# Retention feeding a gated convolutional FFN: units shifted by one token, kept edge columns, one state product moved, and a new written-out order

## The chip, the cores and the metric

The kernel runs on one core of a Trainium2 chip. The metric is the device time of one execution in microseconds, from the core's start to the last output. The core has five engines that run side by side and meet only at semaphores: PE multiplies matrices (PEld is its loading of the stationary matrix), DVE and ACT do elementwise work, POOL does small elementwise work and issues some of the transfers, SP issues the others. Each engine takes its instructions strictly in the order of its queue.

## The reference

Two parts, one feeding the other. The first is retention: for each of 4 batches and 8 heads a 64x64 state is decayed and updated over 768 tokens. The second is a feed-forward net with a convolution of three tokens between its two matrix products.

```python
# retention: q, k, v are (4, 8, 768, 64)
for t in range(S):
    state = gamma * state + outer(k[:, :, t], v[:, :, t])
    y[:, :, t] = scale * einsum('bhd,bhde->bhe', q[:, :, t], state)
x = y.transpose(0, 2, 1, 3).reshape(B, S, H * D)       # (4, 768, 512)
# gated FFN: w_in (512, 1024), conv_w (3, 1024), w_out (1024, 512)
h = maximum(x @ w_in, 0.0)
conv_out[:, s] = sum_k conv_w[k] * h[:, s + k - 1]      # zero outside 0..767
gate = 1 / (1 + exp(-conv_out))
return h * gate @ w_out
```

Because of the convolution, output token s needs h of the tokens s-1, s and s+1.

## The kernel before, in words

**Groups, steps, units.** The four batches go in two groups of two. A group's 768 tokens are 12 steps of 64 tokens, so there are 24 steps; steps 0 to 11 are the first group and 12 to 23 the second. Three steps are a unit: 8 units of 192 tokens and two batches, four to a group. The two first steps are done in a form of their own (both batches of one 128-token piece, `WIDE`).

**A step n.** SP loads q, k, k with tokens first (`kt`) and v, 256 KB each, into one of four `rw` buffers, so the loads of step n can start only when step n-4 is done with its buffer. DVE scales q (`scale_q`, L527) and v (`scale_v`, L533; for early steps ACT does it, L552). One block on PE, `mix(n)`, then interleaves up to three sorts of 64x64 products, two of one sort and two of another in turn: the scores of step n+1 (into `ps_s`), the state's update by step n (into `ps_st`), and step n's output y (into `ps_yo`), which is one part for the first step of a group and two (masked scores times v, old state times q) for the others. Scores and state products use the two straight quadrants of the array ("straight"), y products the two crossed ones ("across"). DVE masks the scores (`masked`, L628), ACT copies the state into the next step's buffer (`carry`, L636). ACT and DVE split y into a rounded head and a rest (`x_head` L654, `x_rest` L659) in the unit's x tile `xu`, since each product of the net is made as three: head by head, head by rest, rest by head.

**A unit u.** For each of 8 column blocks f of w_in, PE makes h with 12 matmuls (`mm1(u, f)`, L738) into a `ps_m` bank, 388 columns wide: two batches of 192 tokens and one token on either side. To have those, each x tile holds 194 tokens; `halo` (L667, ACT) copies one column of x from the neighbouring unit's tile, and `x_tiles` (L643, POOL) writes zeros where the sequence ends. ACT takes h out of the bank with `relu` (L754) and multiplies by the middle tap (`conv_tap`, L767), DVE adds the two outer taps (`conv_side`, L772), ACT makes the sigmoid (`gate`), DVE multiplies (`gated`), and both split the result (`g_head`, `g_rest`) in a `g` tile. For each pair of blocks PE then makes its part of the output (`mm2`, L804, 6 matmuls of 512 columns for each of three 128-token tiles). ACT copies a tile out of its bank (`put`, L812) into one of four `t` buffers and POOL issues its transfer (`out`, L824); the last unit's go by SP. Unit 0 is computed before unit 1's first column of x is there, so `edge` (L759, ACT) later copies one column of h from unit 1 to unit 0.

**What sets the order.** A table of strings, `ORDER`, has one letter for each task of each engine, in the order in which the engine gets them; DMA is the order of loads on SP. `plan` replays these strings with estimated durations to hand out buffers and to place warming matmuls where PE would be idle early on; it changes no order within an engine. At most eight loads are under way (`fetch`, L450): each waits for the one eight before it to land.

Of the kernel before, what the change touches and what calls it, by code (L numbers as in the profile page):

```python
# [21 lines left out]
P = 128  # L22
C = 64
# [23 lines left out]

WIDE = 2
# [44 lines left out]
}  # L93
COLD = 6400
HOP, HOP_PE, SWITCH = 40, 65, (85, 190)
DMA_FIRST, DMA_BYTE, DMA_LAND, DMA_ISSUE, DMA_DEPTH = 1030, 1 / 395, 1030, 450, 8
FETCH, FETCH_NS, BEHIND, PACKET_LAG = (112.6, 126.6), (600, 2300), 500, {2: 700, 6: 1200, PE: 1000}
FIRST = {PE: 6700.0, DVE: 1200.0, ACT: 3200.0, POOL: 2500.0, DMA: 700.0}
# [31 lines left out]
def list_tasks():  # L130
# [22 lines left out]
    for n in range(N_STEPS):  # L153
# [19 lines left out]
        else:  # L173
# [13 lines left out]
            count = 32 + 32 * (c > 0) + 32 * both + 32 * (c + 1 < NC)  # L187
            pe(("mix", n), 1935, after, [("ps_yo", ("y", n))] + [("ps_s", n + 1)] * both, [("rw", n)], count)
        if n >= WIDE - 1 and c + 1 < NC:
            task(("carry", n), ACT, act(512, 45), [("state" if wide else "mix", n), ("load_q", n + 1)])  # L190
        if n == first:
            task(("x_tiles", u), POOL, (60, 120), [u and ("x_tiles", u - 1)], [("xu", u)])
        task(("x_head", n), ACT, act(512, 45), [("mix", n), ("x_tiles", u)])
        done = ("x_rest", n)
        task(done, DVE, tt(512), [("x_head", n)], free=[("ps_yo", ("y", n))])
        if n + 1 == first + width and c + 1 < NC:
# [718 lines left out]
```

## Time and profile before

| | |
|---|---|
| time, median of 3 runs | 347.95 us (347.15 to 348.5) |
| the profiled execution | 347.51 us, of which the span from first to last instruction is 345.8 us |
| PE busy | 335.7 us, 97% of the span |
| DVE, ACT, POOL busy | 205.3, 189.2, 18.4 us |
| granted TensorE clock | 1.00 |

The profile is of one execution. Its time is 0.44 us below the median of the runs, and 1.7 us of it lie outside the span. Busy is the time in which an engine has at least one instruction under way; matmuls overlap, so PE's busy share says that it is never without work for long, not that it works at its best rate. What ends its idle times is in the waits.

### The profile page before, as it was taken

How to read it: one execution, taken by the hardware profiler on the slowest of the kernel's cores; microseconds unless marked ns; L12 is line 12 of the kernel's file. 1: busy time of each engine (PE TensorE's matmuls, PEld its weight loads, DVE VectorE, ACT ScalarE, POOL GpSimd, SP SyncE). 2: the span in 40 equal slices, each digit the busy share in tenths (PEclk: the TensorE clock that was granted, in tenths of full speed). 3: DMA queues.
4: the chain of work that ended last, by engine and by line, in shares of the span. 5: the costliest groups of instructions: out<-in, count | busy, mean ns of one | idle time of the engine just before them, and what ended most of it. 6: DMA issues, size and time to landing. Idle time of an engine off the chain costs nothing.

```text
span 345.8 us, 9832 instructions
## 1 busy us (share of the span) xinstructions
PE 335.7 (97%) x4317; PEld 299.3 (87%) x4317; DVE 205.3 (59%) x318; ACT 189.2 (55%) x381; POOL 18.4 (5%) x45
## 2 busy tenths in 40 slices
PE   8789999999999999999999999999999999999996
PEld 5689899988989898889889988989899899998885
DVE  2756658887899875556921667834806641573540
ACT  1858997676775756365440667454327352453432
POOL 2000000000000001001000010020001000100200
PEclk9999999999999999999999999999999999999999
DMA  7988895766752322157005201020001000200203
GB/s 219 381 291 272 264 330 173 233 221 211 254 180 90 95 93 61 39 179 234 11 2 190 85 14 51 0 61 35 0 32 32 30 2 0 61 2 30 73 21 91
DMA packets 20935, 40.15 MB, mean 116 GB/s; under 512 B 2854, under 2 KB 3116, under 8 KB 20892
## 3 DMA queue, kind: packets, MB, share of 16 engines
q1 hardware_dynamic: 19100, 34.01, 29.5%
q0 software_dynamic: 1792, 5.51, 5.1%
q8 instruction: 34, 0.56, 0.6%
q14 instruction: 9, 0.07, 0.1%
HBM read 33.21 MB, written 6.29 MB: 114 GB/s over the span
## 4 chain that ended last, share of the span: by engine, by line
PE 85%; DMA 7%; SPq 2%; DVE 2%; issue 1%; ACT 1%; DVEq 0%; ACTq 0%
PE ps_yo L804 39%; PE ps_m L738 34%; PE ps_s L577 5%; PE ps_yo L577 4%; PE ps_st L577 4%; DMA rw<-in_qk 3%; SPq L450 2%; DMA w<-in_w_out 1%; DMA rw<-in_kv 1%; DMA w<-in_w_in 1%; DVE hc L772 1%; DVE rw L527 1%; ACT top L702 0%; ACT rw L552 0%; DVE g L791 0%
## 5 line engine op out<-in xcount | busy, mean ns | idle before, releaser
L738 PE MATMUL ps_m<-xu,w 128*128 128x388 f32 (+2 forms) x780 | 145.3, 339 | 0.5 <-issue 0.4
L804 PE MATMUL ps_yo<-w,g 128*128 128x512 f32 (+1 forms) x600 | 140.9, 386 | 0.1
L738 PEld LDWEIGHTS ps_m<-xu,w 128*128 128x128 f32 x780 | 136.2, 188 | 4.5 <-issue 0.6
L804 PEld LDWEIGHTS ps_yo<-w,g 128*128 128x128 f32 x600 | 108.6, 188 | 22.0 <-issue 0.4
L772 DVE SCALAR_TENSOR_TENSOR hc<-hc,cw_sb,hc 128x384 f32<-128x384 f32 x128 | 74.8, 612 | 59.9 <-ACT hc L767 58.6
L754 ACT ACTIVATE hc<-ps_m 128x388 f32<-128x388 f32 x64 | 31.1, 491 | 50.7 <-PE ps_m L738 48.6
L577 PE MATMUL ps_yo<-rw 64*64 64x64 f32 (+1 forms) x1408 | 47.8, 221 | 0.1
L577 PEld LDWEIGHTS ps_yo<-rw 64*64 64x64 f32 (+1 forms) x1408 | 43.9, 135 | 0.8 <-issue 0.5
L767 ACT ACTIVATE hc<-hc,cw_sb 128x384 f32<-128x384 f32 x64 | 38.3, 613 | 5.8 <-DVE g L791 5.6
L791 DVE TENSOR_TENSOR g<-hc,g 128x768 fp32r<-128x768 f32 x32 | 30.5, 953 | 17.9 <-ACT g L786 17.9
L786 ACT CAST g<-hc 128x768 fp32r<-128x768 f32 x32 | 26.5, 833 | 26.6 <-PE ps_yo L804 21.1
L782 DVE TENSOR_TENSOR hc<-hc,hc 128x768 f32<-128x768 f32 x32 | 30.3, 951 | 7.4 <-ACT hc L777 7.3
L777 ACT ACTIVATE hc<-hc 128x768 f32<-128x768 f32 x32 | 26.9, 845 | 13.8 <-DVE hc L772 13.8
L577 PEld LDWEIGHTS ps_s<-rw 64*64 64x64 f32 (+1 forms) x720 | 24.6, 136 | 9.6 <-issue 6.3
L577 PE MATMUL ps_s<-rw 64*64 64x64 f32 (+1 forms) x720 | 28.3, 223 | 2.9 <-DVE rw L626 1.1
L812 ACT COPY t<-ps_yo 128x512 f32<-128x512 f32 (+1 forms) x25 | 14.1, 566 | 26.2 <-PE ps_yo L804 26.1
L824 POOL DMA_DIRECT2D out_y<-t x28 | 15.5, 557 | 220.7 <-ACT t L812 183.4
L659 DVE TENSOR_TENSOR xu<-ps_yo,xu 128x512 fp32r<-128x512 f32 x24 | 16.3, 684 | 14.8 <-ACT xu L654 14.8
L577 PE MATMUL ps_st<-rw 64*64 64x64 f32 (+1 forms) x672 | 23.8, 219 | 1.1 <-issue 1.0
L577 PEld LDWEIGHTS ps_st<-rw 64*64 64x64 f32 (+1 forms) x672 | 21.8, 135 | 1.6 <-issue 1.2
L654 ACT CAST xu<-ps_yo 128x512 fp32r<-128x512 f32 x24 | 14.2, 591 | 9.5 <-PE ps_yo L577 7.6
L628 DVE TENSOR_TENSOR rw<-ps_s,mask 128x512 f32<-128x512 f32 x22 | 15.0, 684 | 5.2 <-PE ps_s L577 5.2
(44 smaller groups left out, 135.5 us busy)
## 6 DMA issues: line engine op xcount, KB each, us to landing
rw<-in_qk SPq DMA_DIRECT2D x48, 256.0 KB, 4.0
rw<-in_kv SPq DMA_DIRECT2D x46, 256.0 KB, 4.9
w<-in_w_in SPq DMA_DIRECT2D x16, 256.0 KB, 4.8
w<-in_w_out SPq DMA_DIRECT2D x16, 256.0 KB, 4.9
out_y<-t POOLq DMA_DIRECT2D x14, 256.0 KB, 2.3
out_y<-t POOLq DMA_DIRECT2D x14, 128.0 KB, 2.5
out_y<-t SPq DMA_DIRECT2D x4, 128.0 KB, 2.3
out_y<-t SPq DMA_DIRECT2D x1, 256.0 KB, 2.3
```

The costliest lines, as they stand in the source:

```text
L577: nc.tensor.matmul(out, lhsT, rhs, start=start, stop=stop, skip_group_check=True)
L659: nc.vector.tensor_tensor(out=lo, in0=y_of(n), in1=hi.bitcast(F32), op=ALU.subtract)
L738: nc.tensor.matmul(ps, w[:, k], x[:, k], start=first and i == 0, stop=(i == len(products) - 1), skip_group_check=True)
L754: nc.scalar.activation(h, buf("ps_m", (u, f))[:, : G * (UNITS[u] * C + 2)], AF.Relu)
L767: nc.scalar.activation(cv, h, AF.Copy, scale=w)
L772: nc.vector.scalar_tensor_tensor(out=cv, in0=h, scalar=w, in1=cv, op0=ALU.mult, op1=ALU.add)
L777: nc.scalar.activation(cv, cv, AF.Sigmoid)
L782: nc.vector.tensor_tensor(out=cv, in0=h, in1=cv, op=ALU.mult)
L786: nc.scalar.copy(g_of(u, p)[:, 0], cv_of(u, 2 * p))
L791: nc.vector.tensor_tensor(out=lo, in0=cv_of(u, 2 * p), in1=hi.bitcast(F32), op=ALU.subtract)
L804: nc.tensor.matmul(ps, g, w[:, cs], start=(f == 0 and i == 0), stop=(f == NF - 1 and i == 2))
L824: (nc.sync if u == LAST[0] else nc.gpsimd).dma_start(out[r0 : r0 + n, columns(u, t, h)], o[at - t * P : at - t * P + n])
```

## The change

The unit boundaries move. A unit's mm1 now covers the tokens of `TOKENS` (0 to 192, 192 to 385, 385 to 577, 577 to 768 in the first group; 0 to 193, 193 to 385, 385 to 577, 577 to 768 in the second), each token once, instead of 194 for each unit. The outputs of a unit remain the same 192 tokens. The columns of h that the next unit needs at its left, one or two (`LEFT`), are copied on POOL into a small tile (`keep`, new) and from there into the next unit's h tile (`left`, new). `halo` and `x_tiles` are gone. `edge` moves from ACT to POOL. Where a unit's first step lends its first token to the unit before (five steps), `x_head` and `x_rest` are two instructions each instead of one. The state product of step 12 moves from mix(12) to mix(11). All strings of `ORDER` are new, and some of `plan`'s constants (which also decide how many warming matmuls there are; their number is the same).

```diff
+TOKENS = [(0, 192), (192, 385), (385, 577), (577, 768), (0, 193), (193, 385), (385, 577), (577, 768)]
+PER = S // (UNITS[0] * C)
+LEFT = [TOKENS[u][0] - FIRST_STEP[u] % NC * C + 1 for u in range(len(UNITS))]
...
     "Pool": (
-        "xxxxxxooooooxoxoooooooooooooo"
+        "kkeleeeeelkeklklkklellklkkkkooolllolkklkoolkokooolloolkkkkolollolkoklkoollooo"
     ),
...
+def states_with(n):
+    if n == NC:
+        return []
+    return [NC] if n == NC - 1 else [n] * (n % NC + 1 < NC)
...
-        straight += list(of_state(n)) if n % NC + 1 < NC else []
+        straight += [product for m in states_with(n) for product in of_state(m)]
...
-    @emits
-    def x_tiles(u):
-        x, first, end = x_of(u), FIRST_STEP[u], FIRST_STEP[u] + UNITS[u]
-        t = UNITS[u] * C + 2
-        for edge in [0] * (first % NC == 0) + [t - 1] * (u == 0 or end % NC == 0):
-            nc.gpsimd.memset(x[:, :, :, :, edge : edge + 1].bitcast(F32), 0.0)
...
+        t = n % NC * C - TOKENS[u][0]
+        if t >= 0:
+            return [(y, [x_of(u)[:, i, :, :, t : t + C] for i in range(2)])]
+        parts = [(y[:, :, :, -t:], [x_of(u)[:, i, :, :, : t + C] for i in range(2)])]
+        return parts + [(y[:, :, :, :-t], [x_of(u - 1)[:, i, :, :, t:] for i in range(2)])]
...
-    @emits
-    def halo(n, du):
...
-        nc.scalar.copy(flat(x_of(u + du))[:, :, dst : dst + 1], flat(x_of(u))[:, :, src : src + 1])
...
     def relu(u, f):
-        h = h_of(u, f)[:, f % 2].rearrange("p b t -> p (b t)")
-        nc.scalar.activation(h, buf("ps_m", (u, f))[:, : G * (UNITS[u] * C + 2)], AF.Relu)
+        t = TOKENS[u][1] - TOKENS[u][0]
+        h = h_of(u, f)[:, f % 2, :, LEFT[u] : LEFT[u] + t]
+        nc.scalar.activation(h, buf("ps_m", (u, f))[:, : G * t].rearrange("p (b t) -> p b t", b=G), AF.Relu)
...
     def edge(f):
 
-        nc.scalar.copy(h_of(0, f)[:, f % 2, :, -1:], h_of(1, f)[:, f % 2, :, 1:2])
+        nc.gpsimd.tensor_copy(h_of(0, f)[:, f % 2, :, -1:], h_of(1, f)[:, f % 2, :, 1:2])
+
+    def kept(u, p):
+        return edge_sb[:, p, :, :, : LEFT[u]]
+
+    @emits
+    def keep(u, p):
+
+        at = UNITS[u] * C
+        nc.gpsimd.tensor_copy(kept(u + 1, p), h_of(u, 2 * p)[:, :, :, at : at + LEFT[u + 1]])
+
+    @emits
+    def left(u, p):
+        nc.gpsimd.tensor_copy(h_of(u, 2 * p)[:, :, :, : LEFT[u]], kept(u, p))
 
     def taps(u, f, k):
-        return h_of(u, f)[:, f % 2, :, k : k + UNITS[u] * C], cv_of(u, f)[:, f % 2], cw_sb[:, f, k : k + 1]
+
+        t0, t1 = int(u % PER == 0 and k == 0), UNITS[u] * C - int(u % PER == PER - 1 and k == 2)
+        return h_of(u, f)[:, f % 2, :, k + t0 : k + t1], cv_of(u, f)[:, f % 2, :, t0:t1], cw_sb[:, f, k : k + 1]
```

In POOL's string k is keep, l is left, e is edge and o is out: 24 keeps, 24 lefts, 8 edges, 21 outs. Nine times a left stands directly behind an out. Three places of the queues follow.

**PE, mix(11) and mix(12).** Before, mix(11) ends with y products alone, since the group's last step updates no state:

```order
L577 MATMUL ps_s_1429<-rw_1135 64x64 x2
L577 MATMUL ps_yo_1428<-rw_1034 64x64 x2
L577 MATMUL ps_s_1429<-rw_1135 64x64 x2
L577 MATMUL ps_yo_1428<-rw_1034 64x64 x18
L738 MATMUL ps_m_1481<-xu_164,w_1050 128x388 x12
```

and mix(12) ends with state products alone:

```order
L577 MATMUL ps_s_1547<-rw_1238 64x64 x2
L577 MATMUL ps_yo_1546<-rw_1135 64x64 x2
L577 MATMUL ps_st<-rw_1135 64x64 x16
L804 MATMUL ps_yo_1602<-w_1240,g_1368 128x512 x3
L804 MATMUL ps_yo_1602<-w_1346,g_1368 128x512 x3
```

In the changed kernel the state products of step 12 (`rw_1136`) lie among mix(11)'s y products; the order's last pairs of mix(11) are

```order
L592 MATMUL ps_st<-rw_1136 64x64 x2
L592 MATMUL ps_yo_1456<-rw_1012 64x64 x2
L592 MATMUL ps_st<-rw_1136 64x64 x2
L592 MATMUL ps_yo_1456<-rw_1012 64x64 x2
L825 MATMUL ps_yo_1528<-w_1372,g_1164 128x512 x3
```

and mix(12) ends with its last pair of scores and y. The 16 products that moved no longer have a stretch of their own. Mix(11) now needs step 12's `kt` and scaled v, and one more mm1 block stands ahead of it than before (unit 1's last, which stood behind it).

**SP, the loads around step 13's k.** The tile `rw_1135` is step 12's, `rw_1238` step 13's, `rw_1370` step 14's and `rw_1495` step 15's buffer; the last can be written only once mix(11) is done. Before:

```order
L450 DMA rw_1135<-in_qk 128x512
L450 DMA w_1274<-in_w_out 128x1024
L450 DMA rw_1370<-in_qk 128x512
L450 DMA w_1274<-in_w_out 128x1024
L450 DMA rw_1135<-in_kv 128x512
L450 DMA w_1380<-in_w_out 128x1024
L450 DMA rw_1495<-in_qk 128x512
L450 DMA w_1380<-in_w_out 128x1024
L450 DMA rw_1238<-in_kv 128x512
L450 DMA rw_1238<-in_qk 128x512
```

and in the changed kernel, where `rw_1136`, `rw_1253`, `rw_1395` and `rw_1536` are the buffers of steps 12 to 15:

```order
L465 DMA rw_1136<-in_qk 128x512
L465 DMA w_1262<-in_w_out 128x1024
L465 DMA w_1338<-in_w_out 128x1024 x2
L465 DMA rw_1253<-in_qk 128x512
L465 DMA rw_1136<-in_kv 128x512 x2
L465 DMA w_1370<-in_w_out 128x1024 x2
L465 DMA rw_1395<-in_qk 128x512
L465 DMA rw_1536<-in_qk 128x512
```

Step 13's k stood behind step 15's q; now it stands ahead of it, and so do step 12's kt and v.

**SP, the start.** The loads from the eleventh on; `rw_173` (before) and `rw_175` (after) are step 2's buffer. Before, step 2's q, step 1's v, step 2's k, step 3's q:

```order
L450 DMA rw_152<-in_kv 128x512
L450 DMA w_169<-in_w_in 128x1024
L450 DMA rw_173<-in_qk 128x512
L450 DMA rw_154<-in_kv 128x512
L450 DMA rw_173<-in_qk 128x512
L450 DMA rw_197<-in_qk 128x512
```

and after, step 2's q, its v, step 3's q, step 2's k:

```order
L465 DMA rw_162<-in_kv 128x512
L465 DMA w_168<-in_w_in 128x1024
L465 DMA rw_175<-in_qk 128x512
L465 DMA rw_175<-in_kv 128x512
L465 DMA rw_192<-in_qk 128x512
L465 DMA rw_175<-in_qk 128x512
```

Step 2's k has moved back by one place, behind step 3's q.

## Rows read from the trace of the kernel before

**Rows 1.** The page: busy time of PE, and the granted clock in 40 slices.

```profile
PE 335.7 (97%) x4317; PEld 299.3 (87%) x4317; DVE 205.3 (59%) x318; ACT 189.2 (55%) x381; POOL 18.4 (5%) x45
...
PEclk9999999999999999999999999999999999999999
```

**Rows 2.** Busy us of each engine by stage, then clock and DMA share.

```profile
0.00:21.00 21.00, 16.55 (x368) 12.84 (x372) 10.42 (x17) 9.22 (x21) 2.50 (x14) 1.00 0.90 306
21.00:70.00 49.00, 48.33 (x1222) 45.39 (x1213) 33.23 (x54) 38.95 (x97) 0.13 (x1) 1.00 0.78 257
70.00:100.00 30.00, 28.50 (x434) 25.79 (x433) 25.67 (x41) 22.88 (x48) 0.13 (x1) 1.00 0.62 213
100.00:342.00 242.00, 241.88 (x2311) 214.98 (x2310) 136.00 (x207) 117.61 (x216) 15.66 (x29) 1.00 0.18 58
```

**Rows 3.** The chain that ended last, two late stretches: start, duration, piece.

```profile
256.02 10.60 PE ps_m L738 x60
...
304.69 4.17 PE ps_yo L804 x18
```

**Rows 4.** PE in order of time, 30 to 90 us: start, duration, group, idle before.

```profile
30.67 0.27 PE L577 MATMUL ps_s<-rw 64*64 64x64 f32 x2
...
32.69 2.39 PE L738 MATMUL ps_m<-xu,w 128*128 128x388 f32 x12
...
76.77 0.27 PE L577 MATMUL ps_s<-rw 64*64 64x64 f32 x2 [0.86 <-DVE rw L628]
...
78.79 4.50 PE L738 MATMUL ps_m<-xu,w 128*128 128x388 f32 x24
...
85.33 0.33 PE L577 MATMUL ps_s<-rw 64*64 64x64 f32 x4 [0.64 <-DMA rw<-in_qk]
...
86.39 1.04 PE L577 MATMUL ps_st<-rw 64*64 64x64 f32 x30
87.36 1.67 PE L804 MATMUL ps_yo<-w,g 128*128 128x512 f32 x6
```

**Rows 5.** SP in order of time: start, duration, issue.

```profile
70.53 0.43 SPq L450 DMA_DIRECT2D w<-in_w_out  x1
78.94 0.33 SPq L450 DMA_DIRECT2D rw<-in_qk  x1
...
80.27 0.91 SPq L450 DMA_DIRECT2D rw<-in_qk  x2
```

**Rows 6.** The chain that ended last, between 65 and 86 us: start, duration, piece.

```profile
65.13 4.74 DMA w<-in_w_out
...
80.27 4.92 DMA rw<-in_qk
```

**Rows 7.** The load of step 2's k, alone in its window.

```profile
L450 SPq DMA_DIRECT2D rw<-in_qk x1: 1512/1512/1512, 7.7 to 7.7; - x1
...
DMA to landing us min/median/max: 6.1/6.1/6.1
```

**Rows 8.** PE in order of time, 13 to 21 us.

```profile
13.94 1.15 PE L577 MATMUL ps_s<-rw 64*64 64x64 f32 x32 [1.12 <-DVE rw L626]
...
16.04 0.97 PE L443 MATMUL ps_yo<-warm 128*128 128x512 f32 x3
17.05 0.69 PE L577 MATMUL ps_st<-rw 128*64 128x64 f32 x16
```

**Rows 9.** Groups of small instructions by line and shape: count, busy us, mean ns.

```profile
L667 ACT CAST xu<-xu 128x16 fp32r<-128x16 f32 x11 | 2.4, 218 | 0.8 <-DVE xu L659 0.8
...
L759 ACT COPY hc<-hc 128x2 f32<-128x2 f32 x8 | 1.4, 189 | 0.0
...
L643 POOL MEMSET xu<- 128x16 f32 x5 | 0.6, 128 | 87.7 <-DVE rw L628 61.6 <-PE ps_m L738 16.2 <-issue 9.9
```

**Rows 10.** POOL's transfers, and DVE's largest instruction.

```profile
L782 DVE TENSOR_TENSOR hc<-hc,hc 128x768 f32<-128x768 f32 x32 | 30.3, 951 | 7.4 <-ACT hc L777 7.3
...
L824 POOL DMA_DIRECT2D out_y<-t x28 | 15.5, 557 | 220.7 <-ACT t L812 183.4 <-DVE xu L659 36.8 <-ACT hc L754 0.4
```

More of the change, by code (lines that the diff above doesn't have):

```diff
@@ L89 @@
     "w_bits": "b", "w_rest": "l", "conv_side": "yz", "gated": "d",
[3 rows of a table removed]
[3 rows of a table added]
 }
-COLD = 6400
+COLD = 6200
 HOP, HOP_PE, SWITCH = 40, 65, (85, 190)
 DMA_FIRST, DMA_BYTE, DMA_LAND, DMA_ISSUE, DMA_DEPTH = 1030, 1 / 395, 1030, 450, 8
-FETCH, FETCH_NS, BEHIND, PACKET_LAG = (112.6, 126.6), (600, 2300), 500, {2: 700, 6: 1200, PE: 1000}
-FIRST = {PE: 6700.0, DVE: 1200.0, ACT: 3200.0, POOL: 2500.0, DMA: 700.0}
+FETCH, FETCH_NS, BEHIND, PACKET_LAG = (112.6, 126.6), (600, 2300), 0, {2: 700, 6: 1200, PE: 1000}
+FIRST = {PE: 6200.0, DVE: 1200.0, ACT: 3200.0, POOL: 2500.0, DMA: 700.0}
 WARM_UP, WARM_SMALL, WARM_NS = (4, 1), 51, 232
@@ L186, in list_tasks @@
             after += [c and (("carry", n - 1), -900), both and ("scale_q", n + 1), both and ("load_k", n + 1)]
-            count = 32 + 32 * (c > 0) + 32 * both + 32 * (c + 1 < NC)
-            pe(("mix", n), 1935, after, [("ps_yo", ("y", n))] + [("ps_s", n + 1)] * both, [("rw", n)], count)
+            count = 32 + 32 * (c > 0) + 32 * both + 32 * len(states_with(n))
+            after += [("scale_v", NC), ("load_kt", NC)] if n == NC - 1 else []
+            pe(("mix", n), 960 if n == NC else 1935, after, [("ps_yo", ("y", n))] + [("ps_s", n + 1)] * both, [("rw", n)], count)
         if n >= WIDE - 1 and c + 1 < NC:
[L190 to L196, printed above, removed]
-            task(("halo", n, 1), ACT, (110, 215), [done, n < WIDE and ("x_rest", 0), ("x_tiles", u + 1)])
-        if n == first and c > 0 and u > 1:
-            task(("halo", n, -1), ACT, (110, 215), [done, ("x_tiles", u - 1)])
+            task(("carry", n), ACT, act(512, 45), [("state", n) if wide else ("mix", n - (n == NC)), ("load_q", n + 1)])
+        split = n == first and TOKENS[u][0] % C
+        task(("x_head", n), ACT, act(512, 45 + 200 * bool(split)), [("mix", n)], [("xu", u)] * (n == first))
+        task(("x_rest", n), DVE, tt(576 if split else 512), [("x_head", n)], free=[("ps_yo", ("y", n))])
     for i in [*range(NF), CONV, *range(NF, CONV)]:
@@ L214, in list_tasks @@
         n0, n1 = FIRST_STEP[u], FIRST_STEP[u] + width
-        body, cols = G * width * C, G * (width * C + 2)
-        x = [("x_tiles", u)] + [("x_rest", n) for n in range(n0, n1)]
-        x += [n0 % NC and ("halo", n0 - 1, 1), u and n1 % NC and ("halo", n1, -1)]
+        body, cols = G * width * C, G * (TOKENS[u][1] - TOKENS[u][0])
+        x = [("x_rest", n) for n in range(n0, n1 + (TOKENS[u][1] % C > 0))]
         for f in range(NF):
@@ L225, in list_tasks @@
                 n = G * P
-                after = [("w_rest", f), f and ("mm1_wide", f - 1), ("x_tiles", 0), ("x_rest", 0), ("x_rest", 1)]
+                after = [("w_rest", f), f and ("mm1_wide", f - 1), ("x_rest", 0), ("x_rest", 1)]
                 pe(("mm1_wide", f), 12 * matmul(n), after, take, count=12)
@@ L230, in list_tasks @@
             task(("relu", u, f), ACT, act(cols, 50), [("mm1", u, f)], [] if odd else [h], [("ps_m", (u, f))])
+            left = u % PER and ("left", u, p)
+            if not odd and left:
+                task(left, POOL, (120, 260), [("relu", u, f), ("keep", u - 1, p)])
+            if odd and u % PER < PER - 1:
+                task(("keep", u, p), POOL, (120, 260), [("relu", u, f), left])
             if u == 1:
-                task(("edge", f), ACT, (110, 215), [("relu", 1, f), ("relu", 0, f)])
+                task(("edge", f), POOL, (120, 260), [("relu", 1, f), ("relu", 0, f)])
             tap = ("conv_tap", u, f - 1) if f else u and ("conv_tap", u - 1, NF - 1)
-            task(("conv_tap", u, f), ACT, act(body, 187), [("relu", u, f), ("w_bits", CONV), tap], [] if odd else [cv])
-            task(("conv_side", u, f, 0), DVE, stt(body), [("conv_tap", u, f)])
+            after = [("relu", u, f), ("w_bits", CONV), tap, LEFT[u] > 1 and left]
+            task(("conv_tap", u, f), ACT, act(body, 187), after, [] if odd else [cv])
+            task(("conv_side", u, f, 0), DVE, stt(body), [("conv_tap", u, f), left])
             task(("conv_side", u, f, 2), DVE, stt(body), [("conv_side", u, f, 0), u == 0 and ("edge", f)])
@@ L271, in plan @@
     slots = {name: {i: 0.0 for i in range(n)} for name, n in BUFS.items()}
-    bus, narrow, lag, count, border, fetched, landings = 0.0, True, 0.0, 0, FETCH[0], 0.0, []
+    bus, narrow, lag, count, border, fetched, packet, landings = 0.0, True, 0.0, 0, FETCH[0], 0.0, -9e9, []
     def earliest(k):
```

53 lines of the change are left out of this document (26 added, 27 removed), and 6 rows, old and new, of the table LETTER.

## The prediction

> **What bounds the kernel now.** I read the page first. PE is busy 97% of the span and its clock stays at the full level in all 40 slices [rows 1], so the kernel is bound by PE's work and by the few microseconds in which PE has none. The stretches show where those are [rows 2]: until 21 us PE is busy 16.55 of 21, from 21 to 70 us 48.33 of 49, from 70 to 100 us 28.50 of 30, and from 100 to 342 us 241.88 of 242. So after 100 us the time is PE's own work: removing a matmul there pays in full, and DVE (136.0 of 242) and ACT (117.6) can lose microseconds for nothing, as long as no wait of PE comes to hang on them. Between 70 and 100 us DVE is busy 25.67 of 30; there an extra wait on DVE can reach PE.
>
> Next I read PE in order of time for what ended its idle stretches [rows 4]. Two stand in the stretch from 70 to 100 us: 0.86 us ahead of mix(11), until DVE had masked the scores, and 0.64 us ahead of mix(12), until a load of q or k landed. The chain [rows 6] and SP's order [rows 5] tell the second one's story. SP issues nothing from 70.53 + 0.43 to 78.94 us, because the load at its head, step 15's q, needs the buffer that mix(11) frees at 78.79 [rows 4]. Step 13's k stands behind it, is issued at 80.27 and lands 4.92 us later, at 85.19; mix(12) starts at 85.33. At the start, scores(2) begins at 13.94 [rows 8]. The profile names DVE as what ended that wait, but step 2's k, issued at 7.74 with 6.1 us to landing [rows 7], is in at 13.84, which fits as well.
>
> **The change, part by part.**
>
> *Fewer columns.* The eight unit widths are 384, 386, 384, 382, 386, 384, 384, 382 columns, 3072 together; before they were 8 x 388 = 3104. That is 32 columns less for each of 8 blocks x 12 matmuls, 3072 columns in all. Their price is the slope between two full stretches [rows 3]: 4.17 us / 18 = 231.7 ns for 512 columns, 10.60 / 60 = 176.7 ns for 388, so 55 ns / 124 = 0.4435 ns a column and **1.36 us**. The whole quotient 176.7 / 388 bounds it above (1.40); a saving of nothing would need matmuls that don't follow their columns, which the two rows exclude.
>
> *The state product of step 12.* In mix(12) the 16 state products stand alone from 86.39 to the next block at 87.36 [rows 4]: 0.97 us. In mix(11) they go between y products that stand alone there now. Would mix(11) get longer? Mix(11) now takes 76.77 to 78.79, 2.02 us, with 48 products; mix(4), with both quadrant pairs filled throughout (64 products), takes 30.67 to 32.69, also 2.02 us [rows 4]. So the moved products ride free. **0.97 us**, between 0 (if they don't) and 0.97.
>
> *Waits at mix(11) and mix(12).* In the new order of SP, step 13's k is ahead of the loads that need mix(10)'s and mix(11)'s buffers, so it is issued without that halt, some 9 us sooner: the 0.64 us go. Mix(11) now waits for more, step 12's kt and its scaled v, but one mm1 block (4.50 / 2 = 2.25 us [rows 4]) has moved in front of it, which is more than the 0.86 us that it waited. Against that, DVE has to scale step 12's v ahead of it, and mix(12) is only half as long now and comes soon after: its masked scores have 1.39 us of mm2 (4.17 / 3 [rows 3]) and 2.02 us of mix(11) to be ready in, while DVE has other work of some 3 to 4 us between (five or six instructions of 0.6 to 0.95 us, the largest in [rows 10]). I take 0.4 us of new wait there: 1.50 - 0.4 = **1.1 us** gained, between 0 and 1.5.
>
> *The start.* Step 2's k is one load later. At the 306 GB/s of the first stretch [rows 2] a piece of 256 KB takes 0.86 us; that mean has the first landings' delay in it, so I take 0.6 us by which scores(2) starts later. Behind it stand mix(1), the warming matmuls (0.97 us, unchanged) and state(1), which now starts at 17.05 [rows 8]. The delay is partly taken up further on, because the first mm1 block and mix(3) wait for DVE's x_rest and masked of steps 1 to 3, not for PE. I take a **loss of 0.3 us**, between 0 and 0.7.
>
> *Off the path.* ACT loses 11 halos (2.4 us) and 8 edges (1.4 us) and gains five small x_head pieces, about 0.2 us each by the halo's 218 ns [rows 9]. DVE gains five pieces, 1 us. Both have room outside 70 to 100 us [rows 2]. POOL loses five memsets and gains 56 copies of 2 to 16 elements a partition. No copy of POOL is in the trace; the nearest rows are its memset of 16 elements, 128 ns, and ACT's copy of two elements, 189 ns [rows 9], so 7 to 11 us on an engine that is busy 18 us. I cost them at nothing, because they run while DVE and ACT work on earlier blocks. What that hides is priced below: each `left` is now ahead of the first outer tap on DVE, and where two columns are kept, ahead of ACT's middle tap.
>
> *The remaining order.* Every string is new. Late, PE has no waits to lose [rows 2], so it can only get worse; the number of changes between small and large matmuls, the other price of an order, is 43 in both of PE's strings, so I cost it at nothing, with up to 1 us of loss in the range.
>
> *Sum.* 1.36 + 0.97 + 1.1 - 0.3 = 3.1 us. The profiled execution took 347.51 us, so 344.4; the median of the runs is 0.44 above it, so 344.8 us.
>
> **The rivals.**
>
> *The waits come back elsewhere* (0.22). Only the work leaves, 2.33 us, and new waits or the start eat the rest: 347.95 - 2.33 = 345.6, up to 346.4. For it: 1.5 us of waits is little against a wholly new order. Against it: late stretches had 0.12 us of waiting in 242, so PE's queue is deeply covered there.
>
> *POOL and DVE hold each other up* (0.15). Of the 56 copies some 12 to 20 fall between 70 and 100 us by the queue. If each holds DVE for its own 0.13 to 0.2 us, DVE loses 2 to 4 us of the 4.3 it has free there, the waits of mix(11) and mix(12) stay and grow, and the gain of 1.1 becomes a loss of about 1.5: 344.8 + 2.6 = 347.4, no change. Against it: before, POOL did nothing but memsets and transfers, so no row shows either way. The Trainium skill (SBUF — State Buffer, Who interferes with whom) has a rule for this: a DVE instruction with two SBUF inputs and a GpSimd instruction that reads SBUF exclude each other for a whole instruction, and one that only writes is free of it. DVE's taps, gated and g_rest all read two SBUF tiles, and the new copies read, unlike the memsets; by that rule the time is this rival's 347.4. No run so far shows it.
>
> *POOL's queue holds the net up* (0.10, slower). Nine times a left stands directly behind an out in POOL's queue. An out waits for ACT's put, and POOL waited 220.7 us ahead of 28 of them, 7.9 us each, then issues for 0.55 us [rows 10]. Until it goes, the left waits, with it DVE's first tap, and behind that on DVE the scaled v, masked scores and x_rest of coming steps, for which PE waits. One exposed wait of the mean length gives 344.8 + 7.9 = 352.7. It decides from 5 us exposed in all. Against it: units are computed long before they are used (36 mm2 blocks stand ahead of unit 3's first in PE's string), so a late left meets slack.
>
> *Everything goes* (0.08). The start loses nothing and no new wait comes: 347.95 - 1.36 - 0.97 - 1.5 = 344.1, and 0.6 of the other early waits too: 343.5.
>
> **How the numbers follow.** The forecast has 0.45, with a range of its own from 344.0 to 345.8. Half a per cent, 1.7 us, is about what a measurement can tell here; faster means under 346.2, slower over 349.7. Faster: 0.45 + 0.08 + 0.17 of the first rival = 0.70. Same: the rest of the first, 0.05, and 0.14 of the second: 0.19. Slower: 0.10 and 0.01: 0.11. The range from 343.0 to 347.6 leaves out the slow rival and the tails of the others, about 0.18.
>
> **What would show it.** mm1 blocks of 12 in a full stretch at 2.10 us or less instead of 2.12; mix(12) about 1.0 us and mix(11) still 2.0; step 13's k landed by 76 us and no wait for a load ahead of mix(12); scores(2) at about 14.6. If DVE's taps wait for POOL in the waits, or DVE's gated gets longer than 951 ns, the second or third rival is at work. I am wrong if PE shows waits of over a microsecond after 100 us, or if the early stretch up to 100 us does the same blocks no sooner.

## The result, and the profile after

The changed kernel takes 344.12 us in the median of four runs (343.27 to 345.03); the kernel before, beside it on the same chip, 348.12 us in four runs. The ratio is 0.989, with a 95% interval from 0.986 to 0.992. Measured again later beside other versions it took 344.05 against 347.24, 0.990 (0.988 to 0.992). Predicted were 344.8 us. The profiled execution took 345.03 us with a span of 343.3; before it was 347.51 with 345.8.

The page answers to [rows 1]: PE's busy time is 3.3 us less, and POOL's, 18.4 us before, has more than doubled.

```profile
PE 332.4 (97%) x4317; PEld 297.4 (87%) x4317; DVE 204.2 (59%) x323; ACT 185.7 (54%) x367; POOL 41.5 (12%) x96
```

The stretches answer to [rows 2] (span, then busy us of PE, PEld, DVE, ACT and POOL, each with its count, then clock, DMA share and GB/s):

```profile
0.00:21.00 21.00, 15.82 (x347) 12.62 (x348) 9.73 (x17) 10.28 (x26) 2.40 (x12) 1.00 0.89 295
21.00:70.00 49.00, 47.02 (x1223) 44.34 (x1222) 32.57 (x54) 36.31 (x86) 2.73 (x8) 1.00 0.72 247
70.00:100.00 30.00, 29.88 (x336) 27.98 (x334) 28.55 (x47) 22.71 (x43) 6.73 (x13) 1.00 0.71 245
100.00:340.00 240.00, 239.66 (x2417) 212.43 (x2415) 133.39 (x207) 116.28 (x216) 29.68 (x63) 1.00 0.19 58
```

From 70 to 100 us PE is busy 29.88 of 30, where it was 28.50: both waits of [rows 4] have gone. After 100 us it is without work for 0.34 us in 240. But up to 21 us it is busy for 15.82 us, where it was 16.55, and from 21 to 70 us for 47.02 of 49, where it was 48.33.

PE in order of time shows where (start, duration, group, and in brackets the idle time before it with what ended it; "issue" means that the trace shows nothing that PE waited for):

```profile
15.16 1.15 PE L592 MATMUL ps_s<-rw 64*64 64x64 f32 x32 [2.32 <-DVE rw L641]
...
21.68 0.21 PE L592 MATMUL ps_st<-rw 64*64 64x64 f32 x1 [1.18 <-issue]
...
22.30 0.98 PE L743 MATMUL ps_m<-xu,w 128*128 128x256 f32 x6
...
32.16 0.27 PE L592 MATMUL ps_s<-rw 64*64 64x64 f32 x1 [1.21 <-issue]
...
33.38 4.46 PE L743 MATMUL ps_m<-xu,w 128*128 128x384 f32 x24
37.77 0.27 PE L592 MATMUL ps_s<-rw 64*64 64x64 f32 x2
...
78.60 0.27 PE L592 MATMUL ps_s<-rw 64*64 64x64 f32 x2
...
80.47 0.67 PE L592 MATMUL ps_yo<-rw 64*64 64x64 f32 x3
81.06 1.67 PE L825 MATMUL ps_yo<-w,g 128*128 128x512 f32 x6
82.66 0.27 PE L592 MATMUL ps_s<-rw 64*64 64x64 f32 x2
...
83.75 1.68 PE L825 MATMUL ps_yo<-w,g 128*128 128x512 f32 x6
```

Scores(2) starts at 15.16, 1.22 later than in [rows 8]; the first mm1 block at 22.30; mix(4) halts for 1.21 us just ahead of 32.16; mix(5) starts at 37.77. Mix(11) runs from 78.60 to 81.06 with all its products, mix(12) from 82.66 to 83.75. (Each 64x64 product that the prediction counts is two matmuls in the trace: mix(4) has 64 of the one and 128 of the other.) For the same points of the kernel before, which [rows 4] do not hold, three more of its lines:

```profile
21.30 0.87 PE L738 MATMUL ps_m<-xu,w 128*128 128x256 f32 x5
...
35.02 0.27 PE L577 MATMUL ps_s<-rw 64*64 64x64 f32 x2
...
46.32 0.86 PE L738 MATMUL ps_m<-xu,w 128*128 128x388 f32 x4 [0.40 <-issue]
```

The chain that ended last, two late full stretches and its end, answers to [rows 3]:

```profile
274.04 6.26 PE ps_m L743 x36
...
301.20 4.17 PE ps_yo L825 x18
...
339.70 0.37 ACT t L833
```

With PE's end at 339.70 us (342.52 before, by the same view) the two profiled executions divide as follows.

| stretch on PE | before | after | difference |
|---|---|---|---|
| start to the first mm1 | 21.30 | 22.30 | +1.00 |
| first mm1 to mix(5) | 13.72 | 15.47 | +1.75 |
| mix(5) to PE's end | 307.50 | 301.93 | -5.57 |

The work up to mix(5) is the same in both but for the columns, so +1.75 is waiting: 1.42 us at the halt of mix(4) and 0.27 at a smaller one in mix(3), each the step from one matmul to the next less the median step of its kind. The last stretch loses the columns (1.3), the state product (0.97), the two waits (1.50) and also six small halts, 0.18 to 0.56 us, that the kernel before had there at 36, 38, 41, 46, 67 and 168 us, 1.8 us in all; a new one of 0.33 us stands in mix(11) ahead of 80.8 us. That is some 5.2 of the 5.57; 0.3 us stay unassigned. Of the six halts the trace names no releaser for those at 36, 41 and 46 us, 1.1 us together; the other three end on ACT or DVE.

POOL's copies and DVE's largest groups in the groups by line and shape (count, busy us, mean ns of one, idle before them) answer to [rows 9, 10]:

```profile
L774 POOL COPY edge_sb<-hc 128x8 f32<-128x8 f32 x20 | 10.1, 520 | 61.8 <-ACT hc L760 61.8
L778 POOL COPY hc<-edge_sb 128x8 f32<-128x8 f32 x20 | 8.0, 405 | 76.8 <-DVE hc L803 39.4 <-DVE g L812 19.5 <-ACT rw L651 18.0
...
L793 DVE SCALAR_TENSOR_TENSOR hc<-hc,cw_sb,hc 128x384 f32<-128x384 f32 x96 | 56.0, 611 | 27.4 <-ACT hc L788 27.3
...
L803 DVE TENSOR_TENSOR hc<-hc,hc 128x768 f32<-128x768 f32 x32 | 30.2, 952 | 4.2 <-ACT hc L798 4.2
```

In these rows a keep takes 520 ns in the mean and a left 405, not the 128 to 189 of the estimate; all 56 copies keep POOL busy for 24.8 us. DVE's taps take 611 ns and gated 952 ns (951 before): DVE is no slower. POOL and DVE in order of time at 73 to 75 us show why:

```profile
73.67 0.66 POOL L778 COPY hc<-edge_sb 128x4 f32<-128x4 f32 x1
74.27 0.67 POOL L774 COPY edge_sb<-hc 128x4 f32<-128x4 f32 x1
75.05 0.41 POOL L765 COPY hc<-hc 128x2 f32<-128x2 f32 x1
75.40 0.18 POOL L774 COPY edge_sb<-hc 128x4 f32<-128x4 f32 x1
```

```profile
73.60 0.68 DVE L729 TENSOR_TENSOR w<-t,w 128x512 fp32r<-128x512 f32 x1
74.20 0.68 DVE L548 TENSOR_TENSOR rw<-rw,const_sb 128x512 f32<-128x512 f32 x1
74.81 0.61 DVE L793 SCALAR_TENSOR_TENSOR hc<-hc,cw_sb,hc 128x384 f32<-128x384 f32 x1
```

The left that begins at 73.67 ends at 74.33, 0.05 us after DVE's instruction from 73.60 has ended; the keep from 74.27 ends at 74.94, 0.05 after the next one. The keep at 75.40 begins as DVE finishes and takes 0.18.

### The profile page after: what moved, and what is told of

The parts are those of the page before. It is cut to its first block, busy times and chain, and to the rows that moved or that the text cites. A ratio compares the mean times of both kernels' runs of the same rounds, so it can differ in the third digit from the quotient of the medians.

```text
span 343.3 us, 9900 instructions
## 1 busy us (share of the span) xinstructions
PE 332.4 (97%) x4317; PEld 297.4 (87%) x4317; DVE 204.2 (59%) x323; ACT 185.7 (54%) x367; POOL 41.5 (12%) x96
## 4 chain that ended last, share of the span: by engine, by line
PE 94%; DMA 3%; issue 1%; SPq 1%; DVE 0%; ACT 0%
PE ps_m L743 40%; PE ps_yo L825 39%; PE ps_s L592 6%; PE ps_st L592 5%; PE ps_yo L592 4%; DMA rw<-in_qk 1%; DMA xu<-in_rows 1%; SPq L465 1%; PE ps_yo L458 0%; DVE rw L641 0%; ACT t L833 0%; DVE rw L542 0%
## 5 line engine op out<-in xcount | busy, mean ns | idle before, releaser
L743 PE MATMUL ps_m<-xu,w 128*128 128x384 f32 (+4 forms) x780 | 143.5, 337 | 0.0
L793 DVE SCALAR_TENSOR_TENSOR hc<-hc,cw_sb,hc 128x384 f32<-128x384 f32 (+1 forms) x128 | 74.6, 611 | 43.1 <-ACT hc L788 43.0
L760 ACT ACTIVATE hc<-ps_m 128x384 f32<-128x384 f32 (+2 forms) x64 | 31.1, 490 | 72.3 <-PE ps_m L743 61.4
L672 DVE TENSOR_TENSOR xu<-ps_yo,xu 128x512 fp32r<-128x512 f32 (+2 forms) x29 | 16.8, 593 | 15.5 <-ACT xu L667 15.5
L667 ACT CAST xu<-ps_yo 128x512 fp32r<-128x512 f32 (+2 forms) x29 | 14.4, 516 | 19.0 <-PE ps_yo L592 11.4
L774 POOL COPY edge_sb<-hc 128x8 f32<-128x8 f32 (+1 forms) x24 | 11.8, 502 | 97.8 <-ACT hc L760 97.8
```

The source lines that it names most:

```text
L672: nc.vector.tensor_tensor(out=lo, in0=y, in1=hi.bitcast(F32), op=ALU.subtract)
L743: nc.tensor.matmul(ps, w[:, k], x[:, k], start=first and i == 0, stop=(i == len(products) - 1), skip_group_check=True)
L760: nc.scalar.activation(h, buf("ps_m", (u, f))[:, : G * t].rearrange("p (b t) -> p b t", b=G), AF.Relu)
L793: nc.vector.scalar_tensor_tensor(out=cv, in0=h, scalar=w, in1=cv, op0=ALU.mult, op1=ALU.add)
```

## The experiments

Medians are of the runs given; "before" is the kernel before, measured beside it on the same chip.

| version | median us (runs) | before | ratio, 95% |
|---|---|---|---|
| changed kernel | 344.12 (4) | 348.12 | 0.989, 0.986 to 0.992 |
| changed kernel again | 344.05 (6) | 347.24 | 0.990, 0.988 to 0.992 |
| early start | 343.82 (6) | 347.57 | 0.988, 0.985 to 0.992 |
| early start again | 343.12 (6) | 347.24 | 0.989, 0.986 to 0.992 |
| state product back | 343.44 (6) | 347.57 | 0.989, 0.986 to 0.992 |
| copies twice | 343.54 (6) | 347.57 | 0.988, 0.985 to 0.992 |
| before without the two waits | 346.37 (12) | 347.57 | 0.997, 0.994 to 0.999 |
| fewer columns | 338.26 (4) | 347.49 | 0.973, 0.970 to 0.977 |
| mix(4) later | 343.99 (6) | 347.49 | 0.990, 0.988 to 0.993 |
| early start, mix(4) later | 343.15 (6) | 347.49 | 0.989, 0.986 to 0.991 |
| the same, head of w_in sooner | 343.32 (6) | 347.24 | 0.988, 0.985 to 0.991 |
| before, mix(4) sooner | 348.24 (10) | 347.49 | 1.003, 1.001 to 1.006 |

Runs of one version differ by 0.8 to 3.9 us, so a median does not tell a fraction of a microsecond. What each edit did is read from the places in its trace, one profile a version. The strings in the diffs below are cut to the part that differs.

**The price of a column.** The full form of mm1 is cut in eleven of its twelve products.

```diff
-            nc.tensor.matmul(
-                ps, w[:, k], x[:, k], start=first and i == 0, stop=(i == len(products) - 1), skip_group_check=True
-            )
+            n = G * t - 16 * (i > 0) if c1 - c0 == t else None
+            nc.tensor.matmul(
+                ps if n is None else ps[:, :n], w[:, k], x[:, k] if n is None else x[:, k, :n],
+                start=first and i == 0, stop=(i == len(products) - 1), skip_group_check=True,
+            )
```

> The changed kernel with the last 16 columns of each full bank left out in 11 of its 12 mm1 products (the first product still writes all), so the last eight tokens' h of one batch in each unit are only partly summed. That is 63 banks x 11 x 16 = 11088 columns. Theory: each column costs 0.4435 ns as between the two full stretches, so 4.9 us less, blocks of twelve in a full stretch at 2.01 us instead of 2.087, and about 339.2 in the median. Rival (steps): the time of a matmul does not follow its columns one by one between 368 and 384, and the blocks stay at 2.08.

The chain that ended last, the same late stretch of 36 matmuls:

```profile
269.90 6.03 PE ps_m L744 x36
```

6.26 became 6.03 us. A matmul has 16 x 11 / 12 = 14.7 columns less in the mean and 0.23 / 36 = 6.4 ns less, 0.436 ns a column, where 0.4435 was taken. Over a longer stretch, matmuls 2069 to 4239 counted from 0, which takes 215.56 us in both profiles of the changed kernel, this version takes 212.59: 2.97 us for 40 blocks of 176 columns, 0.42 ns a column. The median is 5.9 us below the changed kernel's, near the 4.9 expected and within the scatter of both. From 384 to 368 columns the time follows them, as it was taken to.

**The state product of step 12 put back into mix(12).** The estimates of `plan` follow (not shown).

```diff
 def states_with(n):
-    if n == NC:
-        return []
-    return [NC] if n == NC - 1 else [n] * (n % NC + 1 < NC)
+    return [n] * (n % NC + 1 < NC)
```

> The changed kernel with step 12's state product back in mix(12) and everything else of it kept. Theory (the product rides free in mix(11) and costs 0.97 us alone): mix(12) lasts 2.0 us instead of 1.1, mix(11) stays at 2.0 to 2.1, the time rises by 0.95 us to about 345.1. Rival (the room that it leaves is a wait anyway, or mix(11) becomes shorter without it): no rise above 0.3 us.

PE in order of time around mix(11) and mix(12) of this version:

```profile
78.92 0.27 PE L589 MATMUL ps_s<-rw 64*64 64x64 f32 x2
...
80.95 1.67 PE L822 MATMUL ps_yo<-w,g 128*128 128x512 f32 x6
...
83.58 1.04 PE L589 MATMUL ps_st<-rw 64*64 64x64 f32 x30
84.56 1.66 PE L822 MATMUL ps_yo<-w,g 128*128 128x512 f32 x6
```

Mix(11) without the state products takes 2.03 us (78.92 to 80.95), as in the second profile of the changed kernel with them (79.04 to 81.07). Mix(12) has its 1.0 us of state products alone again. So at this place the move is worth the 0.97 us, and the products ride free. From mix(5) to PE's end this version takes 302.4 us, the two profiles of the changed kernel 301.9 and 301.5. The median, 343.44, does not show that microsecond, and the expected rise did not come.

**The two waits alone, in the kernel before.** Step 13's kt and k, with one piece of w_out, go ahead of step 15's q in SP's order, and the masked scores of step 11 stand seven instructions earlier in DVE's; nothing else of the change. Of the DMA string the part that differs (q, k, t and w are loads of q, k, kt and the two weights):

```diff
-wqwvwqwtkkwvq
+wqwvwwtkqkwvq
```

> The kernel before with only two moves in its order: step 13's k, step 13's kt and one piece of w_out are loaded ahead of step 15's q, and DVE masks step 11's scores seven instructions earlier. Columns, state product and all else as before. Theory (the waits ahead of mix(11) and mix(12) were matters of queue order and could be had without the rest): both waits, 0.86 and 0.64 us, are gone, and the time falls by up to 1.5 us, to about 346.6. Rival (the work that was moved back makes the next block wait): the two waits vanish, but others of the same size stand within the next ten blocks, time within 0.5 us of before.

The stretch from 70 to 100 us, in the same columns as above:

```profile
70.00:100.00 30.00, 29.90 (x443) 27.42 (x442) 26.15 (x42) 23.27 (x50) 0.13 (x1) 1.00 0.64 219
```

PE is busy 29.90 of 30: the order of loads and one early DVE instruction remove both waits. The median falls by 1.2 us. From mix(5) to PE's end the profile is 0.85 us shorter than that of the kernel before, since PE waits more elsewhere, for ACT's relu (one 0.39 us at 101.83, one 0.7 at 38.38) and for DVE's x_rest (0.51 at 167.72). The last two places hold short waits in the kernel before as well (0.14 and 0.12 us), and in the last version below the one for x_rest is 0.70, so what of this the edit caused is not shown. In the changed kernel none of them stands.

**POOL's copies.** Each keep, left and edge is issued twice; the keep is shown.

```diff
-        nc.gpsimd.tensor_copy(kept(u + 1, p), h_of(u, 2 * p)[:, :, :, at : at + LEFT[u + 1]])
+        for _ in range(2):
+            nc.gpsimd.tensor_copy(kept(u + 1, p), h_of(u, 2 * p)[:, :, :, at : at + LEFT[u + 1]])
```

> The changed kernel with each keep, left and edge on POOL issued twice over: 56 more copies, about 23 us more of POOL. Theory (the copies are hidden behind work on earlier blocks, and cost the bound engine nothing): time within 0.5 us of the changed kernel, DVE's taps still 611 ns. Rival (POOL's copies hold DVE up, or POOL's queue holds the net up): the time rises by 1 us or more, with DVE's instructions longer or waits of DVE or PE that end on POOL.

The groups by line and shape, lefts and DVE's gated:

```profile
L781 POOL COPY hc<-edge_sb 128x8 f32<-128x8 f32 x40 | 15.2, 381 | 69.1 <-DVE hc L806 34.5 <-ACT rw L651 17.7 <-DVE g L815 15.7
...
L806 DVE TENSOR_TENSOR hc<-hc,hc 128x768 f32<-128x768 f32 x32 | 30.2, 952 | 4.2 <-ACT hc L801 4.2
```

POOL is busy 60.8 us instead of 41.5, gated still takes 952 ns and no wait of PE or DVE ends on POOL; ACT's middle tap waits for a left twice, 2.4 us in all (once, 1.1 us, at 305.6 in the changed kernel). Twice the copies cost nothing that can be seen, so neither rival with POOL shows in the time here. The order of lefts behind outs in POOL's queue was not varied by itself.

**The start.** Step 2's k goes directly behind step 2's q on SP, and one masked of step 1 stands ahead of a scale_q on DVE.

```diff
-qkwrbwqgkvvwqvqkkww
+qkwrbwqgkvvwqkvqkww
```

> The changed kernel with two places of its start put right: step 2's k is loaded straight behind step 2's q (ahead of step 2's v and step 3's q), and DVE masks the second half of step 1's scores ahead of scaling step 3's q. Theory (the wait ahead of scores(2) is the load of step 2's k, which landed at 15.03 in the changed kernel and 13.84 before, and the delay is carried on to the first mm1 at 22.3): scores(2) starts near 13.6 instead of 15.16, the first mm1 near 21.2 instead of 22.3, and the time falls by about 1.1 us, to 343.0. Rival (DVE's order or the later loads take the delay up anyway): scores(2) moves but the first mm1 after step 3 and the end do not, time within 0.3 us of the changed kernel.

PE in order of time:

```profile
20.52 2.96 PE L743 MATMUL ps_m<-xu,w 128*128 128x256 f32 x24
...
30.63 0.27 PE L592 MATMUL ps_s<-rw 64*64 64x64 f32 x1 [1.44 <-issue]
...
36.27 0.27 PE L592 MATMUL ps_s<-rw 64*64 64x64 f32 x2
```

The first mm1 comes at 20.52 us instead of 22.30, mix(5) at 36.27 instead of 37.77. In the second run of this version the first mm1 came at 20.58, and yet mix(5) at 38.81. To see which is which, the changed kernel itself was profiled again beside it:

> The earlier start alone, once more, beside the changed kernel itself on one chip. Theory: first mm1 1 to 1.8 us sooner and the halt at matmul 599 still there, so 0.5 to 1.5 us below the changed kernel's median. Rival: the halt at 599 or another takes the whole gain, medians within 0.3 us.

> The changed kernel itself, to compare with on the same chip: 344.1 in the median, ratio to before 0.989, the halts without a releaser at matmuls 346 and 599 again (they go with the place in the program, not with chance). Rival: the halts were chance; then other matmuls or none.

The changed kernel's second profile, in order of time, and two one-microsecond stretches of it (span, PE busy, granted clock, DMA share, GB/s):

```profile
31.05 0.27 PE L592 MATMUL ps_s<-rw 64*64 64x64 f32 x1 [1.99 <-issue]
...
32.26 6.03 PE L743 MATMUL ps_m<-xu,w 128*128 128x384 f32 x24
```

```profile
31.00:32.00 1.00, 0.95 (x61) 1.00 0.17 57
...
34.00:35.00 1.00, 1.00 (x5) 0.50 0.91 254
```

The halts come behind matmuls 346 and 599 again, so they go with the place. With no edit at all the first mm1 came at 20.39 us, 1.9 sooner than in the first profile, and mix(5), at 38.23, 0.46 later. The halt in mix(4) was 1.99 us instead of 1.21, and behind it the granted clock fell to 0.50, the lower of PE's two levels (1.2 GHz): the next 24 matmuls took 6.03 us instead of 4.46. PE's end is 339.75, against 339.70.

The start of this order of loads scatters: over six profiles of versions that have it the first mm1 is at 20.39 to 22.30 us, mean 21.34; with step 2's k right behind its q 20.52 to 20.70 in four; in three profiles of the old order 20.91 to 21.50, mean 21.24. In all 13 profiles the first mm1 comes 0.62 us after the end of the halt behind 346, so it is that halt, more than step 2's k, that sets it. Of an early first mm1 the first run of the early start kept 1.5 us at mix(5); in its second run and in the second profile of the changed kernel the halt in mix(4) took back all of it and more.

**The halts without a releaser.** Counting PE's matmuls from 0, they come behind the same ones in every version: 346 and 599, sometimes 472, 126 or 127 apart. Between them one packet of 16 KB arrives on the queue that the page calls "q8 instruction". The changed kernel's page has 34 such packets, 0.56 MB:

```profile
q8 instruction: 34, 0.56, 0.7%
```

| profile | behind matmul | packet ends | PE goes on | between |
|---|---|---|---|---|
| before | 346 | 19.18 | 20.68 | 1.50 |
| changed kernel | 599 | 30.53 | 32.16 | 1.63 |
| changed kernel again | 599 | 29.49 | 31.05 | 1.56 |
| early start | 599 | 29.04 | 30.63 | 1.59 |
| copies twice | 599 | 29.88 | 31.40 | 1.52 |
| mix(4) later | 472 | 24.61 | 26.14 | 1.53 |

Over the 20 larger halts at these three places in all profiles PE goes on 1.24 to 1.63 us after the packet's end, however long it had stood. The next three places, some 126 and 127 further on, behave alike. In the 78 crossings of these six places PE never goes on sooner than 1.22 us after its packet's end, and where it gets there more than 1.7 us after that end it does not stop. So what PE lacks is its own next instructions. The halts at 36, 41 and 46 us of the kernel before are at these next three places, 1.27 to 1.49 us after a packet; the one at 80.8 us of the changed kernel ends 1.26 us after one. All seven profiles in which mix(4) holds matmuls 541 to 668 with its data there halt behind 599. The kernel before has a block of twelve large matmuls, 541 to 552, ahead of mix(4). Next the order alone was changed:

```diff
-        "frsgrfsatsatabAaAaAAaAaABBaBA
+        "frsgrfsatsatabAaAAaAaAaABBaBA
```

> The changed kernel with one swap in PE's order: mix(4) stands behind two mm1 blocks (PE's matmuls 553 to 680) instead of one (541 to 668), as it stood before; nothing else. Theory (late code): the packet of PE's instructions that holds matmul 599 is fetched when PE is at about its 541st matmul and is usable 2.5 us later; 58 small matmuls take 1.4 us, so PE runs dry; with a block of twelve large matmuls (2.1 us) in between it does not. Expected: the halt of 1.2 us without a releaser inside mix(4) is gone, no halt at another place, mix(5) starts at about 36.6 us instead of 37.77, and the median is 1 us below the changed kernel's 344.1, about 343. Rival (loads): the fetch is late because the transfers around 30 us fill the DMA engines; the halt then stays at over 1 us wherever the small matmuls stand, and the median stays at 344. Second rival (scores late): masked(5) comes a block later, PE waits for DVE ahead of mix(5) by about the same 1 us, and the median stays.

```profile
26.14 0.27 PE L592 MATMUL ps_st<-rw 64*64 64x64 f32 x2 [1.21 <-issue]
...
36.62 0.27 PE L592 MATMUL ps_s<-rw 64*64 64x64 f32 x2
```

No halt behind 599: the theory holds for the place. But one of 1.21 us appears behind 472 in mix(3), 1.53 us after that packet's end. This execution came there 1.5 us sooner than the first profile, but no sooner than both profiles of the early start and the second of the changed kernel, which lost 0.3 us there or nothing. Their packets had ended at 23.03 to 23.31, this one at 24.61; what made it late is not shown. Mix(5) starts at 36.62, 1.2 us sooner than in the first profile, 1.6 sooner than in the second; the median, 343.99, says nothing of it. With the early start as well:

> The swap of mix(4) together with the earlier start (step 2's k right behind its q on SP, one masked earlier on DVE), which alone gave 343.8. Theory (late code): the start's gain of 1.8 us, and the halt of 1.44 us in mix(4) gone as well: mix(5) at about 35.0 us instead of 36.27, PE's end 1.2 to 1.4 us sooner than with the start alone, the median near 342.5, and the best of all versions. Rival (fixed time): something else, a load or DVE, holds mix(5) near 36.3 whatever stands ahead of it, and a new wait with a releaser shows there; then 343.8 as before.

PE, and ACT ahead of it:

```profile
28.92 2.73 PE L743 MATMUL ps_m<-xu,w 128*128 128x384 f32 x12 [0.71 <-ACT w L724]
31.58 0.27 PE L592 MATMUL ps_s<-rw 64*64 64x64 f32 x2
```

```profile
27.07 1.28 ACT L567 ACTIVATE rw<-rw,const_sb 128x128 f32<-128x128 f32 x4 [1.98 <-DMA rw<-in_kv]
28.26 0.60 ACT L724 CAST w<-t 128x512 fp32r<-128x512 f32 x1
```

Again no halt without a releaser in mix(3) or mix(4), but for 0.11 us in mix(3). Mix(5) is at 36.07, hardly sooner than the 36.27 of the early start alone: the rival is right on that. PE's second mm1 block waits 0.71 us for the head of its w_in block, which stands on ACT behind a scaled v whose load landed at 27.07. One more step:

```diff
-        "qakxwkkvcaxwxavczaAvwcvxwaAc
+        "qakxwkkvcaxwxavczaAwvcvxwaAc
```

> The version with the earlier start and mix(4) one block later, and in ACT's order the rounded head of a w_in block ahead of step 3's scaled v instead of behind it. In the version without this, ACT stood 1.98 us until a load of kv landed at 27.07 us, the head of the block came at 28.26 behind it, and PE's second mm1 block ahead of mix(4) waited 0.87 us for it. Theory (queue): the head's inputs are ready at 26.2, so it goes before the load lands, the block's wait is gone, mix(4) starts at about 30.5 us instead of 31.58, PE's end 337.2 instead of 338.2, median near 342.2. Rival (loads): mix(4) and mix(5) then wait for scaled v, whose loads land one every 0.67 us in this stretch, so PE's end stays at 338 and the median at 343.

ACT of this version, and its stretch from 21 to 70 us:

```profile
26.07 0.62 ACT L724 CAST w<-t 128x512 fp32r<-128x512 f32 x1 [0.69 <-DVE t L712]
26.69 1.28 ACT L567 ACTIVATE rw<-rw,const_sb 128x128 f32<-128x128 f32 x4
```

```profile
21.00:70.00 49.00, 48.55 (x1206) 45.58 (x1205) 33.84 (x59) 38.10 (x90) 2.56 (x8) 1.00 0.77 258
```

The head comes 2.2 us sooner, PE is busy 48.55 of 49, mix(5) is at 34.89, and the execution took 341.91 us with PE's end at 336.73, 3 us ahead of the changed kernel's profiles. Its six runs go from 341.46 to 344.0 with a median of 343.32, though. No version beats the changed kernel by more than the scatter of its runs. Where the profiles scatter is plain, though: in the eight of the changed order whose late part is as in the changed kernel, the work from mix(5) to PE's end takes 301.5 to 302.1 us, while mix(5) starts anywhere from 34.89 to 38.81.

The reverse, in the kernel before:

```diff
-        "rfsgrfsatsatabAaAAaAaAaABBB
+        "rfsgrfsatsatabAaAaAAaAaABBB
```

> The reverse: the kernel before with mix(4) behind one mm1 block instead of two (PE's matmuls 541 to 668), nothing else. Theory (late code): a halt of 1 to 2 us without a releaser appears at about matmul 599 inside mix(4), where the kernel before has none; mix(5) starts 1 us later than its 35.0. At the end it is 0.5 to 1.5 us slower than before, since the waits at mix(11) and mix(12) take up a part. Rival (loads): no new halt, since the loads of the kernel before are in another order; then as before within 0.3 us.

PE, and the DVE instruction that ends just ahead of it:

```profile
29.07 0.33 PE L577 MATMUL ps_s<-rw 64*64 64x64 f32 x4 [0.82 <-PE ps_m L738]
```

```profile
28.28 0.69 DVE L527 TENSOR_TENSOR rw<-rw,gq 128x512 f32<-128x512 f32 x1
```

It is 0.75 us slower in the median (ratio 1.003, above 1 by its interval), as expected, but not by the mechanism. PE waited 0.82 us ahead of mix(4). The row names PE itself; DVE's scaled q of step 5, which mix(4) needs, ended at 28.97, 0.1 us earlier, and fits. By then the packet (its end at 28.00) had come, and PE, which came to 599 some 2.5 us after its end, did not stop there. This one does not tell the theories apart.

## Why the prediction was right, and where not

*Fewer columns, 1.36 us.* Right: 0.42 to 0.44 ns a column where 0.4435 was taken, 1.3 us, and late stretches of 384 columns at 6.26 / 36 x 12 = 2.09 us for twelve, under the 2.10 named.

*The state product, 0.97 us.* Right in place and size: mix(12) takes 1.09 us, and mix(11) 2.03 with the products (second profile) and without them; the 2.46 of the first profile have the 0.33 us halt in them.

*The two waits, 1.1 of 1.50 us.* The mechanism was right: step 13's k, issued at 69.69, landed at 75.99, and the kernel before loses both waits by that order and one DVE instruction. The 0.4 us of new wait ahead of mix(12) was put in without need: mix(12) follows mm2 at once.

*The start, +0.3 us.* Half right. Step 2's k lands later, at 13.91 to 15.03 us in six profiles, at 13.73 to 13.96 with the old order, and "scores(2) at about 14.6" came out as 15.16, in the mean of the six as 14.5. But behind it the prediction has the first mm1 wait for DVE's x_rest; in all 13 profiles it comes 0.62 us after the halt behind matmul 346, so PE's packet sets it. So the size is not one number: the first profile shows +1.00, the second -0.91, the mean of six against three +0.10.

*POOL's copies at nothing.* Right on the path, mis-sized in itself. 24.8 us on POOL, not 7 to 11. A copy that begins with DVE idle takes 179 to 206 ns (15 copies), as the row of ACT's edge, 189 ns, had it; nearly all the rest is waiting for DVE. The second rival took the rule from the Trainium skill (SBUF — State Buffer, Who interferes with whom). The trace agrees on POOL's side: copies that begin inside a DVE instruction with two SBUF inputs end 42 to 51 ns after it, or after a later one (but for three that began in its last 13 ns and took 181 to 184), while three that began under one that reads PSUM took 185 to 190. It does not agree with the price that the rival drew from it. When DVE went from one instruction to the next with a copy waiting, the step was in the mean the same as without one (529 and 530 ns for a tap, 870 and 870 for gated and g_rest): only POOL paid. The third rival, POOL's queue, has nothing for it either: no wait of PE or DVE ends on POOL.

*The remaining order at nothing, up to 1 us of loss.* This is the step that failed, in both directions. Against the one profile of the kernel before, the order took away 1.8 us of small halts, which the prediction had not counted, and put in 1.75 us ahead of mix(5), in other executions more. The zero rested on a count of the changes between large and small matmuls and on the late stretches; the 1.75 us and 1.1 of the 1.8 come from which matmuls stand at PE's packet boundaries early on. The 1.1 is of one execution: in the two edited versions of the kernel before, the same three places cost 0.1 us at most. Gain and loss nearly cancel, so the sum of 3.1 us came near to the 3.2 to 4.0 measured in part by luck. Both kernels' `plan` holds a term for this (`FETCH`, a border every 126.6 matmuls, and `FETCH_NS`), which the prediction did not use; replayed, its estimates stop PE in mix(2), mix(11) and mix(19) of the changed kernel, but not in mix(4).

So the first rival (waits come back elsewhere) was true for the stretch up to mix(5), and "everything goes" for the one behind it; the forecast of 344.8 lies between them, and so does the time. Neither sign that would have made the prediction wrong came: no wait of over a microsecond stands after 100 us, and PE's matmul 1833, up to which both kernels have done as many of each kind, starts at 87.37 us instead of 88.87. At matmul 681, shortly ahead of mix(5), it was still 35.57 instead of 32.69.

## What to carry to other kernels

Where a kernel interleaves tiny matmuls with large ones, a hundred tiny ones use up PE's instructions faster than the next block of them arrives, so count matmuls in the trace to find such a boundary, and try a block of large matmuls just ahead of it. Here that removed one halt at its place and brought no gain that the medians show. A gain early in the program is worth only what the next halt leaves of it: follow the same block through the trace to the end of the kernel before a term is booked. A small copy on POOL may last several times its own length beside DVE's two-input work and still cost nothing, as long as nobody waits for it soon.

## What the runs showed of the hardware

- PE halts at boundaries 126 or 127 matmuls with their weight loads apart, for each of which one packet of 16 KB comes on its instruction queue, and goes on 1.24 to 1.63 us after the packet's end. The Trainium skill (Runtime: NRT & Kernel Launch, Instruction fetch mechanics) has the blocks of 16 KB, and says that crossing a boundary is mostly hidden. The trace agrees with the first and, in stretches of 64x64 products that take 2.0 us for 128 matmuls, not with the second: up to 2.52 us are lost at one. Whether the loads under way delay the packet, and what starts it, stays open.
- After halts of 1.99, 2.22 and 2.52 us in mix(4) the granted clock was at 0.50 for some 3 us and the next 24 matmuls took 6.02 or 6.03 us; after halts of 1.21 to 1.90 they took 4.46 to 4.49.
- A copy on POOL that begins inside a DVE instruction with two SBUF inputs waits for DVE, and not the other way round: a copy grew from 0.19 us to as much as 1.40 us, and DVE lost nothing.
